# Recurrent attention beside a long convolution: five score blocks instead of eight, transposes in accumulator banks, and a larger resident part of one weight chunk

## The chip, the cores and the metric

The kernel runs on one core of a Trainium2 chip. The metric is the device time of one launch in microseconds. The profile comes from one execution of the same program; its times start at the first instruction, and the engines are named TensorE (PE, with its weight loads as PEld), VectorE (DVE), ScalarE (ACT), GpSimd (POOL) and SyncE (SP), which issues most of the loads.

## The reference: what is computed

Two independent halves are written side by side into one output of 2048 x 2048.

Half A is a gated long convolution: `k` is convolved with four taps per channel, multiplied by `v`, convolved over 2048 positions with a filter per channel by Fourier transforms, and multiplied by `q`.

Half B is a recurrence over 64 segments:

```python
for s in range(n_seg):                       # 64 segments of 32 rows
    xs = x[:, s * seg_len:(s + 1) * seg_len, :].copy()
    h = jnp.concatenate([mem, xs], axis=1)   # 8 memory rows + 32 rows = 40 rows
    q = jnp.einsum('btd,dhe->bhte', h, Wq)   # 32 heads of 128
    k = jnp.einsum('btd,dhe->bhte', h, Wk)
    v = jnp.einsum('btd,dhe->bhte', h, Wv)
    scores = jnp.einsum('bhqe,bhke->bhqk', q, k) * scale
    scores = jnp.where(mask[None, None], scores, -1000000000.0)
    p = _softmax(scores, axis=-1)
    o = jnp.einsum('bhqk,bhke->bhqe', p, v)
    o = jnp.einsum('bhte,hed->btd', o, Wo)
    mem = o[:, :M, :].copy()                 # the next segment's memory
    outs.append(o[:, M:, :])
```

A segment can't begin before the last one's first 8 output rows are known. Its weights are 4 matrices of 1024 x 4096 in bf16, 32 MB in all, and they do not fit into the on-chip memory; what does not fit is loaded again in each segment.

## The kernel before, in words

**Stages.** The first 460 us do half A on all engines, and, in its gaps, what of half B does not depend on the recurrence: the keys, queries and values of the last 8 rows of all 64 segments (each segment's 32 rows are kept as 24 and 8, and with the memory rows make up 32 + 8 of the 40). The results go to HBM tensors (`REC`, `VBD`) and come back segment by segment. Resident weight chunks are loaded at the end of this stage. Then comes the loop over 64 segments, whose instructions are written out in the order in which each engine runs them (`tc.manual_schedule()`): within an engine nothing overtakes, and waits across engines are put in by the framework from the tiles that an instruction reads and writes.

**Weights.** The matrices are cut into 64 chunks of 128 x 2048 (512 KB). `ORDER` is the order in which a segment uses them; 16 of them (`STREAM`) are streamed through a ring of five buffers `wring`. `fetch` issues the next load on SP as soon as `done` has freed a buffer. Two streamed chunks (`KEPT_A`, `KEPT_B`) are loaded once and kept in unused words of PSUM, out of which VectorE copies quarters into SBUF in each segment (`quarter`, `quarter_b`; line 796). One chunk, `PART`, has its first 512 columns resident in `part`; the other 1536 are loaded in each segment (line 722).

**One segment.** The 32 heads are done in two groups of 16, g = 0 and 1.

1. The keys and queries of group 0 are projected into two PSUM banks `acc0` and `acc1` (`Proj.run`, line 948: a chunk is four matmuls that run side by side), copied to SBUF by ScalarE (`evac`, line 957), transposed on TensorE into a bank of their own, `tps` (lines 889, 966), and copied out by VectorE (lines 1066, 1070).
2. The scores go to `S`, 8 blocks of 40 columns: blocks 0 to 3 hold the first 32 queries, four heads each; blocks 4 to 7 hold the last 8 queries of four heads stacked in the rows, so that in each row only one of the four blocks is the row's own head.
3. `softmax_a`: VectorE takes the maximum over all 8 blocks (981) and subtracts it (983), writes the mask into `S` for the next scores (`seed_scores`, 917 and 918), and ScalarE takes the exponential (986).
4. `softmax_b`: sum, reciprocal, multiplication with `rowhead` (1 for the row's own head, else 0), products into `P_pad`, a sum over the four blocks (1003), and four 32 x 32 transposes into `PT` (1008, 1009).
5. Group 1 does the same, interleaved: while VectorE works on group 0's softmax, TensorE projects q1 and then the first chunks of the values. The k1 transposes go to `tps`, the q1 transposes to `acc1` under the name `turned`; ScalarE copies both out (1079, 1082).
6. `attend` multiplies P with the values into `OTp`, ScalarE copies the result out (`evac_o`, 1028), and the output projection (1038) adds it into `yacc` in the banks `acc0` and `acc1`. `Y` is copied out (1128), stored, and its first 8 rows become the next memory (`fill_mem`, 898, 900).

On ScalarE, the order around the two softmaxes is what the code says: q1's evacuation stands behind the first exponential, and the copy of group 0's attention output behind the second:

```python
            E1 = softmax_a()
            pv1 = Proj(2, 1).run(3)
            attend(0, PT0, V0)
            OT0 = evac_o(0)
            PT1 = softmax_b(E1)
```

**POOL** issues DMAs of its own: in the first stage the loads of `v`, copies of streamed chunks and the stores of the x rows (`x_block`, line 604), in the loop `rec`, `VBs` and the output. The descriptors of these DMAs are kept in an SBUF area whose size `SCRATCH` sets.

Of the kernel before, what the change touches and what calls it, by code (L numbers as in the profile page):

```python
# [23 lines left out]
PART = (3, 4, 0)  # L24
# [14 lines left out]
SCRATCH = 1024  # L39
# [383 lines left out]
def b_kernel(ctx: ExitStack, tc, x, mem0, Wq, Wk, Wv, Wo, outb, n_seg, run_a):  # L423
# [168 lines left out]
    def x_block(b):  # L592
# [11 lines left out]
        rec_stores.append(nc.gpsimd.dma_start(REC[:, 4 * b:4 * b + 4, 0:256], xt.rearrange("p s k t -> p s (k t)")))  # L604
# [110 lines left out]
    def fetch():  # L715
        if loads:
            s, ch = loads.pop(0)
            live[s, ch] = k, t = slot()
            if ch in kept:
                nc.sync.dma_start(dst_view(t[:], ch), dram_chunk(ch))  # L720
            elif ch == PART:
                nc.sync.dma_start(t[:, 512:2048], stream_src(ch)[:, 512:2048])
            else:
                nc.sync.dma_start(t[:], stream_src(ch))
# [14 lines left out]
    with c0p:  # L739
# [16 lines left out]
        for g in range(2):  # L756
# [13 lines left out]
            if g == 0:  # L770
# [9 lines left out]
    two = ctx.enter_context(tc.tile_pool(name="b_two", bufs=2, side="right", reuse_waits="tile"))  # L780
# [10 lines left out]
    B_rest = one.tile([128, 192], I32, name="B_rest")  # L791
    B_homes = [[(tpi[:, 1, :], 0)], [(SBi[:, 320:448], 0), (OTi[:, :, 480:512], 128)], [(OTi[:, :, 416:480], 0)],
               [(B_rest[:], 0), (SBi[:, 448:512], 192)]]
# [7 lines left out]
    def quarter_b(q, tag):  # L801
        t = one.tile([128, 256], I32, tag=tag, name="quarter_b")
        w = []
        for home, at in B_homes[q]:
            n = home.shape[1] * (home.shape[2] if len(home.shape) == 3 else 1)
            if home.shape == B_rest[:].shape:
                part = home.bitcast(BF)
            else:
                bits(like(t[:, at:at + n], home), home)
                part = t[:].bitcast(BF)[:, 2 * at:2 * at + 2 * n]  # L810
# [35 lines left out]
    def pieces(ch):  # L846
# [4 lines left out]
        if ch == PART:  # L851
            return [(0, 512, part[:]), (512, 2048, live[now[0], ch][1][:, 512:2048])]
# [19 lines left out]
    part = one.tile([128, 512], BF, name="part")  # L872
    nc.sync.dma_start(part[:], dram_chunk(PART)[:, 0, 0:512])
# [30 lines left out]
    with tc.manual_schedule():  # L904
# [17 lines left out]
        for s in range(n_seg):  # L922
# [37 lines left out]
            def transposes(sb, tiles=False, tp=tps[:, 0, :]):  # L960
# [18 lines left out]
            def softmax_a():  # L979
                mx = two.tile([128, 8], F32, tag="mx", name="mx")  # L980
                nc.vector.tensor_reduce(out=mx[:], in_=S, op=ALU.max, axis=AX.X)  # L981
                E = one.tile([128, 8, 40], F32, tag="E", name="E")
                nc.vector.tensor_tensor(out=E[:], in0=S, in1=mx[:].unsqueeze(2).to_broadcast([128, 8, 40]),  # L983
                                        op=ALU.subtract)
                seed_scores()
                nc.scalar.activation(E[:], E[:], ACT.Exp, scale=scale)  # L986
                return E

            def softmax_b(E):
                ssum = two.tile([128, 8], F32, tag="ssum", name="ssum")  # L990
                nc.vector.tensor_reduce(out=ssum[:], in_=E[:], op=ALU.add, axis=AX.X)
                nc.vector.reciprocal(ssum[:], ssum[:])
                nc.vector.tensor_tensor(out=ssum[:, 4:8], in0=ssum[:, 4:8], in1=rowhead[:], op=ALU.mult)
                nc.vector.tensor_tensor(out=P_pad[:, 0:4, 0:32], in0=E[:, 0:4, 0:32],
                                        in1=ssum[:, 0:4].unsqueeze(2).to_broadcast([128, 4, 32]), op=ALU.mult)
                own = P_pad[:].rearrange("p b k -> p (b k)")[:, 32:320].rearrange("p (i w) -> p i w", w=72)
                nc.vector.tensor_tensor(out=own[:, 0:4, 0:8], in0=E[:, 0:4, 32:40],
                                        in1=ssum[:, 0:4].unsqueeze(2).to_broadcast([128, 4, 8]), op=ALU.mult)
                nc.vector.tensor_tensor(out=E[:, 4:8, :], in0=E[:, 4:8, :],
                                        in1=ssum[:, 4:8].unsqueeze(2).to_broadcast([128, 4, 40]), op=ALU.mult)  # L1000
                nc.vector.tensor_copy(P_pad[:, 4, 32:64].rearrange("p (i t) -> p i t", i=4), E[:, 4:8, 32:40])
                with nc.allow_low_precision("one of the four terms is not zero"):
                    nc.vector.tensor_reduce(out=P_pad[:, 4, 0:32], in_=E[:, 4:8, 0:32].rearrange("p i k -> p k i"),
                                            op=ALU.add, axis=AX.X)
                PT = one.tile([128, 2, 4, 40], BF, tag="PT", name="PT")
                for kb in range(2):
                    ks = slice(32 * kb, 32 * kb + 32)
                    nc.vector.transpose(out=PT[:, kb, :, 0:32], in_=P_pad[:, 0:4, ks])
                    nc.vector.transpose(out=PT[:, kb, :, 32:40], in_=P_pad[:, 4, ks])
                return PT  # L1010

            def attend(g, PT, V):
                for i in range(4):
                    cv = slice(i * 128, i * 128 + 128)
                    for c in range(4):
                        nc.tensor.matmul(OTp[:, c, i * 40:i * 40 + 40], lhsT=V[32 * c:32 * c + 32, cv],
                                         rhs=PT[32 * c:32 * c + 32, 0, i, :], start=(i == 0), stop=False,
                                         tile_position=(32 * c, 0), skip_group_check=True)
                for c in range(4):
                    nc.tensor.matmul(OTp[:, c, 0:160], lhsT=VBs[32 * c:32 * c + 32, g, :],  # L1020
                                     rhs=PT[32 * c:32 * c + 32, 1].rearrange("p i q -> p (i q)"), start=False, stop=True,
# [42 lines left out]
            q0.run(4)  # L1064
            KT0 = keys(0)
            nc.vector.tensor_copy(KT0[:, :, :, 0:32], transposes(k0, True))  # L1066
            q0 = q0.run(2).evac()
            k1 = Proj(0, 1).run(4)
            QT0 = one.tile([128, 4, 4, 32], BF, tag="QT", name="QT")
            nc.vector.tensor_copy(QT0[:], transposes(q0, True))  # L1070
# [8 lines left out]
            nc.scalar.copy(KT1[:, :, :, 0:32], transposes(k1))  # L1079
            turned = transposes(q1, tp=bank(1, "turned")[:].bitcast(BF)[:, 0:512])  # L1080
# [122 lines left out]
```

## Time and profile before

| | us |
|---|---|
| runs | 1789.31, 1791.54, 1793.37 (median 1791.54) |
| the profiled execution: its own time | 1793.29 |
| its span, first to last instruction | 1791.4 |
| TensorE busy | 1681.0 |
| VectorE busy | 1038.7 |
| ScalarE busy | 658.8 |
| GpSimd busy | 301.2 |
| moved by DMA | 623.31 MB, mean 348 GB/s |

A line of the timeline reads: start, duration, engine, line of the kernel, operation, output<-inputs, shapes, number of merged instructions, and in brackets the idle time of the engine before it with what ended it. A line of the waits reads: who waited for whom, microseconds in total, number of times, the longest. Matmul durations are of one instruction in a pipeline: the next starts before the last has ended, so the step from start to start is what a matmul takes of TensorE's time.

### The profile page before, as it was taken

The page shows a single profiled execution, that of the slowest core. Times are in us where ns is not written, and L with a number is a line of the kernel's source. Part 1 is how long each engine was busy: PE and PEld are TensorE (multiplying, and loading weights), DVE is VectorE, ACT ScalarE, POOL GpSimd, SP SyncE. Part 2 cuts the span into 40 slices and gives each one's busy share as a digit, 9 for nine tenths or more (in the row PEclk, how much of TensorE's full clock was granted, in tenths as well). Part 3 has the DMA queues.
Part 4 walks back from the last instruction along what each step waited for, and adds up shares of the span by engine and source line. Part 5 has one row for each costly group of instructions (what it writes and reads, how often), then busy time and mean ns, then how long its engine had stood idle before and what let it go on. Part 6 is the DMA issues. An engine that isn't in the chain of part 4 may idle for free.

```text
span 1791.4 us, 70833 instructions
## 1 busy us (share of the span) xinstructions
PE 1681.0 (94%) x30776; PEld 994.8 (56%) x30776; DVE 1038.7 (58%) x3429; ACT 658.8 (37%) x1157; POOL 301.2 (17%) x563
## 2 busy tenths in 40 slices
PE   6989997798999999999999999999999999999998
PEld 2443333343566666656666666665666666666665
DVE  9926875433555555555555555565555555656555
ACT  6955650001333333333333333333333333333333
POOL 4002342100111111111111111111111111111111
PEclk9999998899999999999999999999999999999999
DMA  9989987998999999999999999999999999999998
GB/s 342 361 324 290 308 285 265 337 315 325 381 359 356 352 369 372 358 350 364 359 359 368 347 363 354 367 366 352 345 355 365 364 363 350 375 362 364 369 364 295
DMA packets 219756, 623.31 MB, mean 348 GB/s; under 512 B 57442, under 2 KB 57586, under 8 KB 219444
## 3 DMA queue, kind: packets, MB, share of 16 engines
q1 hardware_dynamic: 160948, 550.58, 83.6%
q0 software_dynamic: 19104, 45.13, 7.4%
q10 hardware_dynamic: 39392, 23.07, 4.3%
q8 instruction: 241, 3.95, 0.9%
q14 instruction: 71, 0.58, 0.1%
HBM read 563.63 MB, written 57.67 MB: 347 GB/s over the span
## 4 chain that ended last, share of the span: by engine, by line
PE 66%; DMA 19%; DVE 6%; ACT 4%; issue 3%; ACTq 1%; POOL 0%; SPq 0%; POOLq 0%; DVEq 0%
PE acc L948 30%; PE yacc L1038 19%; DMA wring<-WS 14%; PE kb_ps L624 5%; DMA REC<-stage 2%; ACT OT L1028 2%; PE tps L889 2%; ACT s_sb L249 1%; DVE E L983 1%; DVE mx L981 1%; PE tps L966 1%; PE s_ps L247 1%; ACTq L653 1%; PE turned L966 1%; PE vb_ps L765 1%
## 5 line engine op out<-in xcount | busy, mean ns | idle before, releaser
L1038 PEld LDWEIGHTS <-OT 128*64 128x64 bf16 x8255 | 438.8, 109 | 53.6 <-ACT OT L1028 35.6
L948 PEld LDWEIGHTS <-rec 128*32 128x32 bf16 x12288 | 293.7, 96 | 291.3 <-DVE rec L900 41.7
L957 ACT CAST qkv_sb<-acc 128x512 bf16<-128x512 f32 x384 | 224.7, 585 | 514.1 <-PE acc L948 353.0
L948 PE MATMUL acc<-Wres,rec 128*32 128x512 bf16 x3328 | 242.6, 380 | 2.6 <-issue 2.1
L948 PE MATMUL acc<-wring,rec 128*32 128x512 bf16 x2300 | 228.2, 382 | 17.2 <-DMA wring<-WS 14.0
L1038 PE MATMUL yacc<-Wmore,OT 128*64 128x256 bf16 (+1 forms) x2560 | 219.9, 274 | 0.0
L948 PE MATMUL acc<-Wmid,rec 128*32 128x512 bf16 x3072 | 211.3, 379 | 1.0 <-issue 1.0
L1038 PE MATMUL yacc<-wring,OT 128*64 128x256 bf16 x2448 | 194.9, 273 | 6.9 <-DMA wring<-WS 6.9
L1130 POOL DMA_DIRECT2D out_dram<-Y x128 | 64.6, 507 | 487.4 <-ACT Y L1128 484.4
L796 DVE TENSOR_SCALAR quarter<-OTp 128x256 int32<-128x256 int32 x252 | 99.9, 417 | 78.4 <-ACT OT L1028 78.4
L1128 ACT CAST Y<-yacc 128x256 bf16<-128x256 f32 x128 | 47.6, 372 | 256.8 <-DVE quarter_b L796 164.8
L1028 ACT CAST OT<-OTp 128x640 bf16<-128x640 f32 x128 | 87.4, 683 | 143.4 <-PE OTp L1020 143.4
L948 PE MATMUL acc<-pw,rec 128*32 128x512 bf16 x1796 | 132.7, 379 | 1.0 <-issue 1.0
L1066 DVE COPY KT<-tps 128x512 bf16<-128x512 bf16 x64 | 27.2, 425 | 155.0 <-PE tps L889 155.0
L900 DVE CAST rec<-tps 128x32 bf16<-128x32 f32 x128 | 24.5, 192 | 159.1 <-PE tps L898 155.7
L948 PE MATMUL acc<-Wlate,rec 128*32 128x512 bf16 x1536 | 116.4, 379 | 0.0
L884 POOL DMA_DIRECT2D rec<-REC x64 | 36.2, 565 | 448.4 <-PE acc L948 432.7
L981 DVE TENSOR_REDUCE mx<-SB 128x8 f32<-128x320 f32 x128 | 62.9, 492 | 67.1 <-PE SB L975 64.0
L986 ACT ACTIVATE E<-E 128x320 f32<-128x320 f32 x128 | 60.1, 470 | 82.0 <-DVE E L983 82.0
L624 PE MATMUL kb_ps<-XBT,pw 128*128 128x512 bf16 x320 | 82.9, 400 | 1.9 <-DMA pw<-in_B_Wk_dram 1.3
L1038 PE MATMUL yacc<-Wlate,OT 128*64 128x256 bf16 x1024 | 79.1, 276 | 5.4
L932 POOL COPY KT<-rec 128x128 bf16<-128x128 bf16 x128 | 38.8, 303 | 227.2 <-PE SB L975 220.6
(223 smaller groups left out, 2671.5 us busy)
## 6 DMA issues: line engine op xcount, KB each, us to landing
wring<-WS SPq DMA_DIRECT2D x831, 512.0 KB, 6.2
wring<-WS SPq DMA_DIRECT2D x64, 384.0 KB, 5.7
rec<-REC POOLq DMA_DIRECT2D x64, 192.0 KB, 5.7
SK<-s_sb SPq DMA_DIRECT2D x16, 512.0 KB, 4.5
SU<-s_sb SPq DMA_DIRECT2D x16, 512.0 KB, 5.7
Kg<-SK SPq DMA_DIRECT2D x32, 256.0 KB, 4.1
Ug<-SU SPq DMA_DIRECT2D x32, 256.0 KB, 5.5
REC<-stage ACTq DMA_DIRECT2D x16, 512.0 KB, 13.2
```

Of the source, the lines that this page charges most:

```text
L624: nc.tensor.matmul(ps[:], lhsT=ws[kc][:, hl * 128:(hl + 1) * 128], rhs=xbt(kc).rearrange("p s t -> p (s t)"), start=(kc == 0), stop=(kc == 7))
L796: nc.vector.tensor_scalar(out=dst, in0=src, scalar1=0, scalar2=None, op0=ALU.bitwise_or)
L884: nc.gpsimd.dma_start(rec[:], REC[:, s, :])
L932: nc.gpsimd.tensor_copy(KT[:, :, :, 32:40], KBs[:, 128 * g:128 * g + 128].rearrange("p (c i t) -> p i c t", c=4, i=4))
L948: nc.tensor.matmul(self.acc[32 * c:32 * c + 32, :], lhsT=hT[:, ch[1], :], rhs=w[:, 512 * c:512 * c + 512], start=(ch == chs[0]), stop=(ch ...
L957: nc.scalar.copy(sb[:], self.acc[:])
L981: nc.vector.tensor_reduce(out=mx[:], in_=S, op=ALU.max, axis=AX.X)
L986: nc.scalar.activation(E[:], E[:], ACT.Exp, scale=scale)
L1028: nc.scalar.copy(OT[:], o_view)
L1038: nc.tensor.matmul(yacc[f][64 * dh:64 * dh + m, x - o:y - o], lhsT=lhsT, rhs=r, start=(h == (0, 2 * FIRST[-1])[f] and x == o), stop=stop, ...
L1128: nc.scalar.copy(Y[:, 256 * f:256 * f + 256], yacc[f][:, 0:256])
L1130: nc.gpsimd.dma_start(bass.AP(outb.tensor, outb.offset + SEG * s * 2048 + 512 * dh, [[2048, 32], [1, 512]]), Y[64 * dh + NM:64 * dh + 40, :])
```

## The change

Four things are changed together.

- **Resident part.** `part` holds 1280 of the 2048 columns of chunk `PART` instead of 512 (two loads ahead of the loop instead of one), and the load in each segment fetches 768 columns instead of 1536. `part` grows by 1536 bytes per partition.
- **Space for it.** The words `B_rest` (768 bytes), which held the rest of `KEPT_B`'s last quarter in SBUF, go: these 192 words now lie in `tps`, in the columns that the transposes used, and are copied out in each segment as the other quarters are. The descriptor area shrinks from 1024 to 512 bytes, for which the store in `x_block` is cut in two. `E` shrinks from 320 to 256 columns and takes in the small tiles of the softmax.
- **Transposes.** k0's go to bank 0 and q0's to bank 1, each after its own evacuation; the group is `q0.run(2)`, `k0.run(4)`, `q0.run(3)`, k0's transposes, `q0.run(3)`, where it was `run(4)` and `run(2)`. k1's and q1's go to the two halves of bank 1.
- **Softmax.** The four blocks of the last queries are multiplied with `rowhead` and summed into block 4 ahead of the maximum, and the rest of the softmax works on 5 blocks. P is transposed by two instructions instead of four, with `PT` laid out as [head, key half] instead of [key half, head].

```diff
-PART = (3, 4, 0)
+PART, PART_COLS = (3, 4, 0), 1280
-SCRATCH = 1024
+SCRATCH = 512
...
-        rec_stores.append(nc.gpsimd.dma_start(REC[:, 4 * b:4 * b + 4, 0:256], xt.rearrange("p s k t -> p s (k t)")))
+        for h in (0, 2):
+            rec_stores.append(nc.gpsimd.dma_start(REC[:, 4 * b + h:4 * b + h + 2, 0:256],
+                                                  xt[:, h:h + 2].rearrange("p s k t -> p s (k t)")))
...
-                nc.sync.dma_start(t[:, 512:2048], stream_src(ch)[:, 512:2048])
+                nc.sync.dma_start(t[:, PART_COLS:2048], stream_src(ch)[:, PART_COLS:2048])
...
-    B_rest = one.tile([128, 192], I32, name="B_rest")
-               [(B_rest[:], 0), (SBi[:, 448:512], 192)]]
+               [(tpi[:, 0, 64:256], 0), (SBi[:, 448:512], 192)]]
...
-    part = one.tile([128, 512], BF, name="part")
-    nc.sync.dma_start(part[:], dram_chunk(PART)[:, 0, 0:512])
+    part = one.tile([128, PART_COLS], BF, name="part")
+    nc.sync.dma_start(part[:, 0:1024], dram_chunk(PART)[:, 0, :])
+    nc.sync.dma_start(part[:, 1024:PART_COLS], dram_chunk(PART)[:, 1, 0:PART_COLS - 1024])
...
-            def transposes(sb, tiles=False, tp=tps[:, 0, :]):
+            def transposes(sb, bank_of, at=0, tiles=False):
+                tp = bank_of[:].bitcast(BF)[:, at:at + 512]
...
             def softmax_a():
-                nc.vector.tensor_reduce(out=mx[:], in_=S, op=ALU.max, axis=AX.X)
-                nc.vector.tensor_tensor(out=E[:], in0=S, in1=mx[:].unsqueeze(2).to_broadcast([128, 8, 40]),
-                                        op=ALU.subtract)
+                nc.vector.tensor_tensor(out=own, in0=S[:, 4:8, :], in1=rowhead[:].unsqueeze(2).to_broadcast([128, 4, 40]),
+                                        op=ALU.mult)
+                nc.vector.tensor_reduce(out=S[:, 4, :], in_=own.rearrange("p i k -> p k i"), op=ALU.add, axis=AX.X)
+                nc.vector.tensor_reduce(out=mx, in_=S[:, 0:5, :], op=ALU.max, axis=AX.X)
+                nc.vector.tensor_tensor(out=e, in0=S[:, 0:5, :], in1=mx.unsqueeze(2).to_broadcast([128, 5, 40]),
+                                        op=ALU.subtract)
                 seed_scores()
-                nc.scalar.activation(E[:], E[:], ACT.Exp, scale=scale)
+                nc.scalar.activation(e, e, ACT.Exp, scale=scale)
...
-                for kb in range(2):
-                    ks = slice(32 * kb, 32 * kb + 32)
-                    nc.vector.transpose(out=PT[:, kb, :, 0:32], in_=P_pad[:, 0:4, ks])
-                    nc.vector.transpose(out=PT[:, kb, :, 32:40], in_=P_pad[:, 4, ks])
+                nc.vector.transpose(out=PT[:, :, :, 0:32], in_=P_pad[:, 0:4, :])
+                nc.vector.transpose(out=PT[:, :, :, 32:40].rearrange("p i k t -> p k i t"), in_=P_pad[:, 4, :])
...
-            q0.run(4)
+            q0.run(3)
             KT0 = keys(0)
-            nc.vector.tensor_copy(KT0[:, :, :, 0:32], transposes(k0, True))
-            q0 = q0.run(2).evac()
+            nc.vector.tensor_copy(KT0[:, :, :, 0:32], transposes(k0, bank(0, "turned"), tiles=True))
+            q0 = q0.run(3).evac()
             k1 = Proj(0, 1).run(4)
-            nc.vector.tensor_copy(QT0[:], transposes(q0, True))
+            nc.vector.tensor_copy(QT0[:], transposes(q0, bank(1, "turned"), tiles=True))
...
-            nc.scalar.copy(KT1[:, :, :, 0:32], transposes(k1))
-            turned = transposes(q1, tp=bank(1, "turned")[:].bitcast(BF)[:, 0:512])
+            turned = bank(1, "turned")
+            nc.scalar.copy(KT1[:, :, :, 0:32], transposes(k1, turned))
+            turned = transposes(q1, turned, 512)
```

## The prediction

> **What bounds the kernel now.** I read the page first: TensorE carries the chain, with a DMA share.
>
> ```profile
> PE 1681.0 (94%) x30776; PEld 994.8 (56%) x30776; DVE 1038.7 (58%) x3429; ACT 658.8 (37%) x1157; POOL 301.2 (17%) x563
> ...
> PE 66%; DMA 19%; DVE 6%; ACT 4%; issue 3%; ACTq 1%; POOL 0%; SPq 0%; POOLq 0%; DVEq 0%
> ```
>
> Then the stages by windows. The columns are the stretch, its length, the busy times, the granted clock, the DMA share and GB/s.
>
> ```profile
> 0.00:460.00 460.00, 389.88 (x2249) 164.95 (x2253) 283.70 (x595) 183.30 (x275) 96.68 (x121) 0.94 0.91 317
> 460.00:800.00 340.00, 329.86 (x7300) 211.38 (x7296) 191.98 (x721) 121.05 (x225) 54.13 (x117) 1.00 0.98 361
> 1130.00:1460.00 330.00, 320.49 (x7076) 205.76 (x7064) 183.87 (x688) 116.20 (x216) 51.25 (x111) 1.00 0.98 359
> ```
>
> The recurrent loop holds 1327 of 1791 us. There TensorE is 97% busy and the DMA engines 98%: two resources near their ends. The waits from 460 us on tell which one ends last:
>
> ```profile
> PEld L1038 <- ACT OT L1028: 35.0, 61, 0.9
> ...
> PE acc L948 <- DMA wring<-WS: 12.3, 21, 1.1
> ...
> PE yacc L1038 <- DMA wring<-WS: 4.1, 8, 1.2
> ```
>
> TensorE waits only 16.4 us in all for streamed weights, while the loads on SP mostly wait for TensorE to free a ring slot. So TensorE sets the pace and the stream follows closely. The first segment of that timeline has no stream wait: 20.32 us between its two second-half Y copies (459.84 and 480.16 us). The mean of 63 segments is (1787.1 − 459.84)/63 = 21.07 us. The excess, 0.75 us a segment or 47 us, is all that a lighter stream could give back. What a new wait on TensorE costs is read from this segment:
>
> ```profile
> 462.30 0.58 ACT L957 CAST qkv_sb<-acc 128x512 bf16<-128x512 f32 x1 [2.09 <-PE acc L948]
> 462.66 0.39 PE L948 MATMUL acc<-wring,rec 128*32 128x512 bf16 x4
> ...
> 462.94 0.41 PE L889 MATMUL tps<-ident,qkv_sb 128*32 128x128 bf16 x16
> ...
> 463.39 0.42 DVE L1066 COPY KT<-tps 128x512 bf16<-128x512 bf16 x1 [2.31 <-PE tps L889]
> 463.60 0.82 PE L948 MATMUL acc<-Wmid,rec 128*32 128x512 bf16 x12
> ...
> 467.09 0.47 ACT L986 ACTIVATE E<-E 128x320 f32<-128x320 f32 x1 [0.61 <-DVE E L983]
> ...
> 467.74 0.58 ACT L957 CAST qkv_sb<-acc 128x512 bf16<-128x512 f32 x1 [0.18 <-PE acc L948]
> ...
> 468.27 0.40 PE L966 MATMUL tps<-ident,qkv_sb 128*128 128x128 bf16 x4
> ...
> 468.50 0.39 PE L966 MATMUL turned<-ident,qkv_sb 128*128 128x128 bf16 x4
> ...
> 468.75 0.58 ACT L1079 COPY KT<-tps 128x512 bf16<-128x512 bf16 x1 [0.43 <-PE tps L966]
> ...
> 471.38 0.47 ACT L986 ACTIVATE E<-E 128x320 f32<-128x320 f32 x1 [0.60 <-DVE E L983]
> ...
> 471.75 0.67 ACT L1028 CAST OT<-OTp 128x640 bf16<-128x640 f32 x1
> ...
> 472.48 0.63 PE L1038 MATMUL yacc<-Wlate,OT 128*64 128x256 bf16 x8
> ```
>
> One chunk of a projection (four matmuls side by side) occupies TensorE for about 0.22 us here (463.60 to 464.25 is three). From an engine's end to the start that it releases, these rows show some 0.05 us. Of the evacuations, the OT copy ends at 472.42 and TensorE starts at 472.48: already a stall, and it starts right behind the second exponential (471.38 to 471.75). So what delays that exponential delays TensorE one for one.
>
> **The change, part by part (per segment).**
>
> *First transposes, one chunk earlier and in accumulator banks.* The k0 transposes need the k0 evacuation, which ends at 462.88; today a chunk at 462.66 covers that. Now they come where that chunk stood and still start at 462.94. Three chunks follow (463.17 to 463.82), then k1 starts in bank 0, which VectorE's KT copy reads until 463.81: start 463.86 instead of 463.60. Part of it is won back, since the q0 transposes today wait for their evacuation: theirs would start at 464.73 instead of 464.52. Cost 0.21 us; bounds 0.15 (no wait for bank 0) and 0.28 (nothing won back).
>
> *Second transposes, both in bank 1.* The k1 transposes (468.27) went to a bank of their own. Now they need bank 1, thus the q1 evacuation, whose end at 468.32 plus 0.05 gives 468.37: 0.10 us. That evacuation stands behind the first exponential on ScalarE. ScalarE is free for it at 467.09 + 0.37 (the step from the second exponential to the OT copy) = 467.46, 0.28 before it starts. The exponential's start moves by 0.52 and its length shrinks by 0.10 (next part but one), so 0.14 us of that shows. Cost 0.24; bounds 0.10 and 0.40.
>
> *The q1 transposes behind the KT copy.* In the listing of the changed kernel's instructions, the q1 transposes wait for the ScalarE count that the KT copy of k1 reaches, though they write the other half of the bank. In before they wait for nothing late: 468.50 follows 468.27 directly. The KT copy starts 0.48 after the transposes that it reads and takes 0.58; with 0.05 for the release the second four start 1.11 after the first, not 0.23. Everything behind is queued on TensorE: five chunks of pv0, the scores, pv1. Cost 0.88; bounds 0.80 and 0.95. That one bank is guarded as a whole is also seen in before: VectorE's quarter copies of OTp's upper columns wait for ScalarE's OT copy of the lower ones (78.4 us, 63 times). The Trainium skill, PSUM — Partial Sum Buffer, section "PSUM bank collisions raise a hardware error", asks for this: guard by bank and quadrant, not by address. The trace agrees by those 63 waits; guarded by address this part would cost nothing and the sum would be 55 us lower.
>
> *Softmax, front.* Max (0.492) and subtract (0.491) over 320 columns go. In come: a product of 160 columns out of PSUM (0.328, as the seed of 160), a reduce of 160 to 40 (the 128-to-32 one took 0.368; 32 more columns at the 1.07 ns that 0.319 for 160 and 0.491 for 320 give: 0.40), max and subtract over 200 (0.36 each, 120 columns less). Two instructions more bring two more gaps of 0.03. The exponential starts 1.45 + 0.12 = 1.57 after the scores instead of 1.05: 0.52 later, and is 0.10 shorter (at 0.83 ns a column, from ScalarE's 372 ns for 256 and 585 for 512). The OT copy and TensorE's first output matmul behind it are 0.42 later; bounds 0.30 (reduce at the price of a plain 160) and 0.60 (its strided write to PSUM costs more).
>
> *Softmax, back.* Sum and product shrink, four instructions of 0.16 to 0.37 go, two small ones of about 0.17 come, and the four transposes (0.90) become two, which I put at 0.7. The chain gets some 0.7 us shorter, but it frees nothing: the second P is used at 474.78, 0.27 after its last transpose, and attention of group 0 waits for V's evacuation, not for P. Shorter work there costs and gives 0; were the cover gone it would be a loss only if the front's 0.52 exceeded it.
>
> *Kept quarter.* 192 words now need a VectorE copy (0.25 for 128, so 0.32), just ahead of the 64-word copy at 478.46. Both end near 479.0, the matmul reading them starts at 479.34: 0, as long as that 0.3 us lasts.
>
> *Stream.* The partial chunk loads 192 KB instead of 384 KB: one SP load as before, 12.6 MB less over 64 segments. Nothing moves at TensorE beyond its stream waits, plus fetch and queue stalls that the 98% share may cause. What it returns lies between the 16 named and the whole excess of 47 us; with a slower TensorE the share falls to about 0.9, so I take 28, the named ones and somewhat under half of the rest.
>
> *Ahead of the loop.* POOL issues 16 more stores (0.78 us each today, halves near 0.6): 6 us of an engine that idles there between Yre products. SP's part load becomes two and waits for VectorE's last output product rather than TensorE, about 1.5 us later, with the 13 Wv loads queued behind it; the loop's entry waits for stores and Wlate loads from 381 us on, which cover that. Half the descriptor space shows in no row; POOL's issues there keep 7 us and more apart for the most part. I take +1, between −3 and +8.
>
> **Sum.** 0.21 + 0.24 + 0.88 + 0.42 = 1.75 us; 63 segments give 110 (bounds 1.35 and 2.23: 85 and 140; the first segment waits for loads anyway). 110 − 28 + 1 = +83. The profiled execution took 1793.29 us (span 1791.4), 1.75 above the median 1791.54, and 1793.3 + 83 − 1.7 = 1875 us. Measured runs spread by 0.2%, so that is what counts as no change.
>
> **Rivals.**
>
> *Bytes set the time (faster).* The DMA engines are 98% busy at 358 to 361 GB/s in the loop. If transfers were the bound, 12.6 MB less at 360 GB/s would give 35 us: 1757 us. This decides if the added TensorE waits stay inside time that it now spends on the stream, some 0.26 us a segment; they come to 1.75. Against it also: a slice of the page at 381 GB/s, and the segment of 20.32 us. Chance 0.04. The Trainium skill, DMA: Bandwidth & Descriptors, section Specifications, puts the HBM limit of a core near 358 GB/s; by that the 12.6 MB are worth 35 us too, and the loop's rate agrees with the figure, the 381 of that slice does not.
>
> *The KT copy does not hold the q1 transposes.* Then 0.87 remains: 55 − 28 + 1 = +28, 1820 us. For it: the halves are disjoint. Against: the count in the listing. Chance 0.06.
>
> *Longer than forecast.* The strided reduce into PSUM or the restarts of TensorE cost more and little of the stream's excess comes back: 140 − 16 + 8 = +132, about 1922 us. Chance 0.08.
>
> **How the numbers follow.** The forecast has 0.82, its own range 1845 to 1912. Bounds taken against each other give 85 − 47 − 3 = +35 (1826) at the low end; the range 1838 to 1915 leaves out the faster rival, the KT one and part of the long one. Slower by over 0.2%: 0.95; faster 0.04; same 0.01.
>
> **What would show it.** The q1 transposes named as waiting for ScalarE's KT copy, near 0.9 us each; k1's transposes waiting for the q1 evacuation; the wait of L1038's weights for OT near 1.0 us instead of 0.57; stream waits under 5 us; segments near 22.4 us; the loop's rate near 330 GB/s. Wrong it would be if the q1 transposes follow k1's within 0.25 us, or if segments with no added TensorE waits set the end.

## The result, and the profile after

The changed kernel takes 1939.06 us (median; 1934.62 to 1944.53) against 1792.45 us for the kernel before on the same chip: a ratio of 1.0816, 95% interval 1.0778 to 1.0855. The direction was forecast, the size was not: 1939 lies above the range of 1838 to 1915.

The page of the changed kernel gives the busy times and the chain:

```profile
PE 1706.1 (88%) x30776; PEld 1004.7 (52%) x30776; DVE 1034.4 (53%) x3236; ACT 640.1 (33%) x1157; POOL 312.5 (16%) x579
...
PE 53%; DVE 11%; ACT 9%; DMA 7%; issue 5%; ACTq 1%; POOL 1%; SPq 0%; POOLq 0%; DVEq 0%
```

TensorE's share of the chain fell from 66% to 53%, DMA's from 19% to 7%, and what came instead is VectorE, ScalarE and issue. To see where the 146.8 us between the two profiled executions (1940.06 and 1793.29) come from, the span is cut at the end of the first segment, which is the end of the second second-half `Y` copy of ScalarE in the timeline, as in the prediction. It lies at 534.2 us instead of 460.2: **+74 us ahead of the loop**. The 63 segments behind it take 22.22 us in the mean instead of 21.07: **+73 us in the loop**. The shortest segments, which have no stream wait, went from 20.31 to 22.17 us, by 1.86; what the mean has above them (the excess) went from 0.76 to 0.05 us.

The windows of the changed kernel show both halves (stretch, its length, busy times, granted clock, DMA share, GB/s):

```profile
0.00:460.00 460.00, 345.13 (x1598) 134.82 (x1599) 251.30 (x520) 175.16 (x260) 104.77 (x132) 0.87 0.77 264
800.00:1130.00 330.00, 305.55 (x6733) 195.85 (x6729) 176.65 (x621) 108.20 (x209) 48.84 (x105) 1.00 0.94 333
```

In the loop TensorE waits more and the DMA engines move 333 instead of some 360 GB/s, as forecast. In the first 460 us everything fell: TensorE did 345 instead of 390 us of work, the DMA engines moved 264 instead of 317 GB/s. The waits of the changed kernel from 100 to 540 us say who stopped:

```profile
POOL REC L605 <- issue: 55.5, 14, 5.6
PE z_ps L375 <- POOL Yre L366: 48.8, 12, 9.0
...
POOL out_dram L418 <- issue: 19.4, 5, 6.1
...
POOL WS L675 <- issue: 12.2, 4, 6.1
```

The three "issue" rows stand for 87 us in which POOL stood ahead of a DMA of its own with nothing in the profile that it waited for. Before, from 0 to 540 us, there were no such rows for `REC` and `out_dram` and 2.0 us for `WS`, and TensorE waited 2.7 us for `Yre`. POOL's timeline around one block of x shows it, first before and then after:

```profile
162.49 1.15 POOL L366 TENSOR_TENSOR Yre<-pa,pb 128x512 bf16<-128x512 bf16 x1 [1.97 <-DVE pb L361]
165.05 0.78 POOL L604 DMA_DIRECT2D REC<-xt  x1 [1.41 <-DVE xt L603]
165.83 0.55 POOL L679 DMA_DIRECT2D WS<-pw  x1
166.40 1.17 POOL L366 TENSOR_TENSOR Yre<-pa,pb 128x512 bf16<-128x512 bf16 x1
```

```profile
161.67 1.16 POOL L366 TENSOR_TENSOR Yre<-pa,pb 128x512 bf16<-128x512 bf16 x1 [2.97 <-DVE pb L361]
164.12 0.73 POOL L605 DMA_DIRECT2D REC<-xt  x1 [1.29 <-DVE xt L603]
170.06 0.73 POOL L605 DMA_DIRECT2D REC<-xt  x1 [5.21 <-issue]
170.79 0.57 POOL L681 DMA_DIRECT2D WS<-pw  x1
171.38 2.27 POOL L366 TENSOR_TENSOR Yre<-pa,pb 128x512 bf16<-128x512 bf16 x2
```

The second half of the store starts 5.94 us after the first. The trace also tells when each DMA landed. For the first half, which starts at 164.12 us (least, median and longest are of this one store):

```profile
DMA to landing us min/median/max: 5.6/5.6/5.6
```

It landed at 169.75 us, and the second half starts 0.31 us later. The same holds for all 23 waits of the three rows: each ends 0.30 to 0.34 us after the landing of the last POOL DMA that was still on its way. Behind the second half in POOL's order stand the products `Yre`, and TensorE waits for these: 46 us more in named waits than before. How the rest of the 74 us comes about was not traced.

In the loop, the waits of the changed kernel from 460 us to the end answer to those shown of before:

```profile
PEld L1036 <- ACT OT L1026: 69.2, 64, 1.1
...
PE turned L965 <- ACT KT L1078: 46.6, 64, 0.7
PE yacc L1036 <- ACT OT L1026: 37.6, 64, 0.6
...
PE turned L965 <- ACT qkv_sb L955: 12.5, 54, 0.2
...
PE acc L946 <- DMA wring<-WS: 2.3, 4, 1.0
```

The wait for the `OT` copy was 35.0 us before, the stream's 12.3, and the two rows of `turned` are new. One segment's timeline after, in the rows that the prediction costed:

```profile
651.75 0.33 DVE L981 TENSOR_TENSOR E<-SB,rowhead 128x160 f32<-128x160 f32 x1 [0.63 <-PE SB L974]
652.11 0.45 DVE L983 TENSOR_REDUCE SB<-E 128x40 f32<-128x160 f32 x1
652.60 0.37 DVE L984 TENSOR_REDUCE E<-SB 128x5 f32<-128x200 f32 x1
653.00 0.37 DVE L985 TENSOR_TENSOR E<-SB,E 128x200 f32<-128x200 f32 x1
653.40 0.37 ACT L988 ACTIVATE E<-E 128x200 f32<-128x200 f32 x1 [1.20 <-DVE E L985]
653.68 0.57 ACT L955 CAST qkv_sb<-acc 128x512 bf16<-128x512 f32 x1
...
654.30 0.38 PE L965 MATMUL turned<-ident,qkv_sb 128*128 128x128 bf16 x4 [0.24 <-ACT qkv_sb L955]
654.77 0.59 ACT L1078 COPY KT<-turned 128x512 bf16<-128x512 bf16 x1 [0.53 <-PE turned L965]
655.41 0.38 PE L965 MATMUL turned<-ident,qkv_sb 128*128 128x128 bf16 x4 [0.73 <-ACT KT L1078]
```

The exponential starts 1.65 us after the first VectorE operation; k1's transposes start 0.05 us after q1's evacuation (653.68 + 0.57), and q1's follow 1.11 us later, 0.05 after the `KT` copy.

### The profile page after: what moved, and what is told of

Read it like the earlier page. It is cut to its first block, busy times and chain, and to the rows that moved or that the text cites. A ratio compares the mean times of both kernels' runs of the same rounds, so it can differ in the third digit from the quotient of the medians.

```text
span 1938.3 us, 70724 instructions
## 1 busy us (share of the span) xinstructions
PE 1706.1 (88%) x30776; PEld 1004.7 (52%) x30776; DVE 1034.4 (53%) x3236; ACT 640.1 (33%) x1157; POOL 312.5 (16%) x579
## 4 chain that ended last, share of the span: by engine, by line
PE 53%; DVE 11%; ACT 9%; DMA 7%; issue 5%; ACTq 1%; POOL 1%; SPq 0%; POOLq 0%; DVEq 0%
PE yacc L1036 23%; PE acc L946 19%; ACT qkv_sb L955 3%; DMA wring<-WS 3%; DVE SB L983 3%; PE turned L965 3%; DVE E L984 2%; DVE E L985 2%; ACT OT L1026 2%; DVE E L981 2%; ACT KT L1078 2%; PE turned L887 2%; DMA REC<-stage 2%; PE kb_ps L626 1%; ACT E L988 1%
## 5 line engine op out<-in xcount | busy, mean ns | idle before, releaser
L1036 PEld LDWEIGHTS <-OT 128*64 128x64 bf16 x8255 | 438.3, 109 | 78.1 <-ACT OT L1026 69.2
L946 PE MATMUL acc<-Wres,rec 128*32 128x512 bf16 x3328 | 236.3, 380 | 0.2 <-issue 0.2
L1036 PE MATMUL yacc<-Wmore,OT 128*64 128x256 bf16 (+1 forms) x2560 | 219.1, 274 | 0.0
L1036 PE MATMUL yacc<-wring,OT 128*64 128x256 bf16 x2256 | 187.0, 273 | 1.6 <-DMA wring<-WS 1.6
L1036 PE MATMUL yacc<-Wlate,OT 128*64 128x256 bf16 x1024 | 78.8, 276 | 37.6 <-ACT OT L1026 37.6
L981 DVE TENSOR_TENSOR E<-SB,rowhead 128x160 f32<-128x160 f32 x128 | 41.5, 324 | 129.1 <-PE SB L974 129.1
L1064 DVE COPY KT<-turned 128x512 bf16<-128x512 bf16 x64 | 27.2, 425 | 147.2 <-PE turned L887 147.2
L965 PE MATMUL turned<-ident,qkv_sb 128*128 128x128 bf16 x512 | 49.1, 217 | 59.6 <-ACT KT L1078 46.6
L988 ACT ACTIVATE E<-E 128x200 f32<-128x200 f32 x128 | 47.3, 370 | 151.2 <-DVE E L985 151.2
```

The costliest lines, as they stand in the source:

```text
L946: nc.tensor.matmul(self.acc[32 * c:32 * c + 32, :], lhsT=hT[:, ch[1], :], rhs=w[:, 512 * c:512 * c + 512], start=(ch == chs[0]), stop=(ch ...
L965: nc.tensor.transpose(dst, src, ident[:])
L981: nc.vector.tensor_tensor(out=own, in0=S[:, 4:8, :], in1=rowhead[:].unsqueeze(2).to_broadcast([128, 4, 40]), op=ALU.mult)
L988: nc.scalar.activation(e, e, ACT.Exp, scale=scale)
L1036: nc.tensor.matmul(yacc[f][64 * dh:64 * dh + m, x - o:y - o], lhsT=lhsT, rhs=r, start=(h == (0, 2 * FIRST[-1])[f] and x == o), stop=stop, ...
```

## The experiments

The theory after the result: (A) the half outside the loop is the room for POOL's descriptors; (B) the half in the loop is the sum of four TensorE waits that the prediction listed. The rivals: the cut stores themselves, as 16 more issues; one of the waits not being what it seems; and, for the stream, that a lighter stream is what gave time back. The table holds what the timelines of all kernels give: the end of the first segment, the mean of the 63 others, the shortest value that recurs among them, and what the means have above it in all (63 times the difference). The time is the median of the runs; the segments are those of the one profiled execution, whose own time is up to 7 us off that median (1864.20 for e1, 1780.53 for e12, 1771.08 for e11). So means that differ by less than some 0.1 us are not told apart by it, and the first segment's end lies between 459 and 465 us in kernels whose first stage is that of before (before, e6, e8, e11, e12).

| kernel | time, us | runs | first segment ends | mean | shortest | above it |
|---|---|---|---|---|---|---|
| before (profiled) | 1793.29 | 1 | 460.2 | 21.07 | 20.31 | 48 |
| after (profiled) | 1940.06 | 1 | 534.2 | 22.22 | 22.17 | 3 |
| e1_small_ring | 1857.44 | 2 | 534.1 | 21.02 | 20.31 | 45 |
| e2_cut_stores | 1791.32 | 8 | 464.0 | 20.98 | 20.31 | 42 |
| e3_after_ring | 1873.83 | 4 | 466.6 | 22.25 | 22.17 | 5 |
| e4_turns_first | 1895.01 | 1 | 531.2 | 21.56 | 21.48 | 5 |
| e5_ot_first | 1916.57 | 1 | 534.9 | 21.84 | 21.53 | 20 |
| e7_old_softmax | 1915.52 | 1 | 536.0 | 21.81 | 21.50 | 19 |
| e6_less_stream | 1788.48 | 10 | 460.0 | 20.96 | 20.31 | 41 |
| e12_small_load | 1786.94 | 10 | 459.0 | 20.89 | 20.31 | 36 |
| e11_one_load_fewer | 1765.46 | 4 | 464.8 | 20.64 | 20.31 | 21 |
| e8_before_ot_first | 1793.88 | 7 | 461.9 | 21.01 | 20.41 | 38 |
| e9_otp_turns | 1802.19 | 7 | 465.4 | 21.16 | 20.87 | 18 |
| e10_otp_ot_first | 1793.35 | 7 | 461.2 | 20.97 | 20.22 | 47 |

### e1_small_ring and e2_cut_stores: the area, and the stores alone

Both start from the kernel before. e1 has the small area and the cut stores, e2 the cut stores alone; the loop is untouched.

```diff
-SCRATCH = 1024
+SCRATCH = 512            # e1 alone
...
-        rec_stores.append(nc.gpsimd.dma_start(REC[:, 4 * b:4 * b + 4, 0:256], xt.rearrange("p s k t -> p s (k t)")))
+        for h in (0, 2):     # e1 and e2
+            rec_stores.append(nc.gpsimd.dma_start(REC[:, 4 * b + h:4 * b + h + 2, 0:256], ...
```

> The kernel before with only the descriptor area halved (512 bytes) and the x-row stores cut in two; stream, transposes and softmax as before. Theory A (room for descriptors): POOL's second half store waits some 5 us for the first to drain, the Yre products and all behind it are late, and the first segment ends near 534 us instead of 460; the segments stay at 21.07 us; in all about 1866 us (between 1850 and 1880), with over 40 us of POOL's waits ahead of these stores that no engine's work ends. Theory B (the stage's other changes: the larger part load, its wait on VectorE, another interleaving): first segment ends by 470, in all 1790 to 1803 us.

> The kernel before with the x-row stores cut in two, the descriptor area left at 1024 bytes. Theory A (room): 16 more issues of about 0.7 us on an engine with idle time, first segment ends between 458 and 468 us, in all 1790 to 1800 us. Rival A2 (the number of POOL's DMA issues, not the room): first segment ends near 530, in all about 1862 us.

Against before, e1 has a ratio of 1.0405 (1.030 to 1.051), and its first segment ends at 534.1 us, where that of the changed kernel ends. e2 has 1.000 (0.997 to 1.003) and ends its first segment at 464.0. The waits of e1 from 100 to 540 us, and POOL's timeline of e2 around the same block:

```profile
POOL REC L605 <- issue: 57.7, 14, 9.1
...
PE z_ps L375 <- POOL Yre L366: 49.2, 12, 9.1
```

```profile
166.13 1.45 POOL L605 DMA_DIRECT2D REC<-xt  x2 [1.34 <-DVE xt L603]
167.57 0.57 POOL L681 DMA_DIRECT2D WS<-pw  x1
168.16 1.17 POOL L366 TENSOR_TENSOR Yre<-pa,pb 128x512 bf16<-128x512 bf16 x1
```

With the large area the same two halves go out one right behind the other (merged as x2, 1.45 us in all). So the +74 us belong to the size of the area, all of them that show (e2's 3.8 us lie within the spread of that stage), and the number of issues costs nothing that shows. The Trainium skill, DMA: Bandwidth & Descriptors, section "SWDGE vs HWDGE vs iDMA", says that GpSimd writes the descriptors of its DMAs into rings in an area of SBUF, which the DMA engines drain; the runs agree, in that the area's size alone decides whether POOL stands still ahead of these stores for 57.7 us or not at all. That POOL stands until an earlier store has landed is shown by the landing times of the changed kernel. How much the area holds was not measured; it does not go by the bytes of the transfer alone, since the 512 KB copy `WS` goes out right behind the second half of 128 KB.

### e3_after_ring: the changed loop without the small area

The changed kernel with 1024 bytes of area. For the space, `part` holds 1024 columns instead of 1280; the stores stay cut.

```diff
-PART, PART_COLS = (3, 4, 0), 1280
+PART, PART_COLS = (3, 4, 0), 1024
-SCRATCH = 512
+SCRATCH = 1024
```

> The changed kernel with the descriptor area back at 1024 bytes; to make room the resident part holds 1024 columns instead of 1280. Theory (the stage ahead of the loop is lost to room for descriptors alone): first segment ends between 458 and 470 us, the segments stay at 22.2 us, in all 1866 us (1855 to 1878). Rival (the stage is slow for the larger part load and its wait, or for the cut stores): first segment ends above 500 us, in all above 1900.

1873.83 us (1873.37 to 1876.03), ratio 1.0468 (1.0435 to 1.050). The first segment ends at 466.6 us, and the segments are those of the changed kernel, though the stream carries 64 KB more in each. What the area does not cause is 82 us over the 1791.33 of before here, against the forecast's +83. That it comes so close is in part luck: 74 of them are the loop's, for which 82 were forecast, and the first segment ends 6 us later than that of before.

### e4_turns_first: the q1 transposes ahead of the KT copy

The changed kernel; all eight transposes are issued before the copy, so that they no longer wait for it, while the copy now waits for all eight.

```diff
-            nc.scalar.copy(KT1[:, :, :, 0:32], transposes(k1, turned))
+            k1_turned = transposes(k1, turned)
             turned = transposes(q1, turned, 512)
+            nc.scalar.copy(KT1[:, :, :, 0:32], k1_turned)
```

> The changed kernel with the q1 transposes issued straight after k1's, ahead of ScalarE's KT copy, so that they no longer wait for it; the KT copy waits for them instead. Theory (the KT copy's hold of 0.88 us is the largest term of the loop): the q1 transposes follow k1's within 0.25 us, some 0.2 us comes back as a wait of the scores for the QT copy, segments of 21.5 us instead of 22.18 (21.4 to 21.7), the loop 43 us shorter, in all near 1896 us. Rival (the wait only moves to the scores): segments of 22.0 us or more.

The row of a segment in which the two groups of four stand as one:

```profile
712.98 0.61 PE L965 MATMUL turned<-ident,qkv_sb 128*128 128x128 bf16 x8
```

The shortest segment falls by 0.69 us to 21.48, the time by 44 us in one run. The hold is real, though the two halves of the bank are disjoint: it comes from the guard on the bank as a whole. The gain is less than 0.88, and ScalarE's steps tell why: the `KT` copy starts 0.23 us later, since it now waits for all eight transposes, and the step from the V evacuation to the second exponential grew by 0.19. The step from the `KT` copy to the V evacuation, in which the hold lay, fell by 1.11.

### e5_ot_first and e7_old_softmax: the softmax's share

e5 is the changed kernel with the copy of group 0's attention output ahead of the second exponential on ScalarE. e7 is the changed kernel with the softmax of before on 8 blocks (`part` at 1024 columns), P still transposed in two instructions.

```diff
-            E1 = softmax_a()
+            E1 = softmax_a(False)     # e5: without the exponential
             pv1 = Proj(2, 1).run(3)
             attend(0, PT0, V0)
             OT0 = evac_o(0)
+            nc.scalar.activation(E1[1], E1[1], ACT.Exp, scale=scale)
```

> The changed kernel with ScalarE's copy of group 0's attention output issued ahead of the second exponential. Theory (the output projection starts late because that copy stands behind an exponential which the longer softmax front delays): TensorE's first output matmul follows the last value chunk at once, the wait of L1036's weights for OT goes from 1.0 us to near 0 and segments to 21.5 us (21.4 to 21.65), in all near 1895 us. Rival (the softmax of group 1 is itself needed as early): attention of group 1 waits for P, and segments stay above 21.9 us.

> The changed kernel with the softmax of before (8 blocks, maximum and subtraction at once, selection behind), its transposes of P still two instructions; the resident part holds 1024 columns to make room. Theory (the longer front costs 0.42 us at the attention output's copy and 0.14 at the q1 evacuation, and the shorter back gives nothing): segments of 21.6 us instead of 22.18 (21.5 to 21.75), in all near 1902 us. Rival (the front's length is hidden, what it saves behind pays for it): segments of 22.1 us or more.

In e5 the shortest segment falls by 0.64 us, more than the 0.48 that the softmax had cost there, since the copy no longer stands behind an exponential at all. In e7 it falls by 0.67: so the five-block front costs about what was summed for it, 0.42 at the `OT` copy and 0.24 at the second transposes. But both means fall by 0.4 only, and so both forecasts of the segment (21.5 and 21.6) were met by the shortest ones alone. The waits of e5 from 460 us on:

```profile
PEld L1037 <- ACT OT L1027: 26.8, 63, 0.4
PE acc L946 <- DMA wring<-WS: 10.2, 23, 1.1
```

Two fifths of the gain came back as time above the shortest segment: the stream's named waits are back at 10.2 us, and that time at 20 us. e4, with shortest segments as long and the same stream, has 5 us there. Where in the segment TensorE waits seems to decide that; why was not settled.

### e6_less_stream, e12_small_load, e11_one_load_fewer: what a lighter stream returns

All three start from the kernel before. e6 loads 192 KB of the partial chunk instead of 384, e12 64 KB, e11 nothing; the missing columns are multiplied out of another resident chunk, with the same work on every engine.

```diff
-                nc.sync.dma_start(t[:, 512:2048], stream_src(ch)[:, 512:2048])
+                nc.sync.dma_start(t[:, 1280:2048], stream_src(ch)[:, 1280:2048])   # e6; e12: 1792:2048; e11: no load
-            return [(0, 512, part[:]), (512, 2048, live[now[0], ch][1][:, 512:2048])]
+            return [(0, 512, part[:]), (512, 1280, res[3, 5, 0][:, 512:1280]), (1280, 2048, live[now[0], ch][1][:, 1280:2048])]
```

> The kernel before with 192 KB less streamed in each segment and nothing else: columns 512 to 1279 of the partial chunk are not loaded, and another resident chunk's columns are multiplied in their place. Theory (TensorE sets the pace, the stream's return is bounded by the excess of 47 us over the shortest segment): segments of 20.4 to 20.75 us instead of 21.07, 20 to 42 us less, in all about 1760 us. Rival (the stream hardly holds the loop; only the 16 us of named waits come back): segments of 20.8 to 20.9 us, in all 1776 us.

> The kernel before without the load of the partial chunk in any segment: one load of fourteen and 384 KB less, columns 512 to 2047 of that chunk being multiplied from another resident chunk instead. Theory (what holds the mean above the shortest segment is the number of loads in turn through five buffers, each some 6 us from issue to landing, and not their bytes): a mean of 20.5 to 20.7 us instead of 21.0, 20 to 30 us less in all. Rival (it is neither: the excess comes from other fetches and queues): a mean of 20.85 or more, under 10 us less.

> The kernel before, with the load of the partial chunk kept but cut from 384 KB to 64 KB a segment (columns 512 to 1791 of it are multiplied out of another resident chunk, so this part of the output projection is computed with the wrong weights; the work per engine is the same). Two experiments are to be told apart by it: 192 KB less in the same load returned nothing (ratio 0.999), the whole load of 384 KB left out returned 22 us. Theory of the loads: what counts is that a load stands in the row of five buffers, and its bytes hardly count. Then 320 KB less return at most 5 us: about 1785 us, segments 20.9 us in the mean. Theory of the bytes, with a threshold: the stream has to get lighter by more than 192 KB before the stalls go. Then 64 KB left stand near the kernel without the load: about 1770 us, segments 20.7 us. The shortest segment stays at 20.31 us in both.

| left of the load | ratio to before, 95% interval | segments, mean |
|---|---|---|
| 384 KB (before) | 1 | 21.07 |
| 192 KB (e6) | 0.999 (0.997 to 1.001) | 20.96 |
| 64 KB (e12) | 0.998 (0.996 to 1.000) | 20.89 |
| no load (e11) | 0.988 (0.984 to 0.992) | 20.64 |

Half of the load taken away returned nothing that can be told from zero, less than either theory had put on it. Five sixths of its bytes taken away returned 0.2%, some 4 us, at the edge of what can be told from zero; the load left out returned 1.2%, some 22 us (14 to 28), so that the last 64 KB with the load itself are worth some 18. The rows of DMA issues of e12 (KB each, us to landing):

```profile
wring<-WS SPq DMA_DIRECT2D x831, 512.0 KB, 6.1
wring<-WS SPq DMA_DIRECT2D x64, 64.0 KB, 4.9
```

A load of 64 KB needs 4.9 us to land, one of 384 KB needed 5.7. So in this loop a load costs, and its bytes hardly. That it is its place in the row of five buffers that costs is argued, not shown: in e11 TensorE's named stream waits fell from 16.6 to 4.0 us, and the waits of its weight loads for nothing that the profile names fell too, while e12 has 13.9 and 35.9 us:

```profile
PEld L948 <- issue: 34.8, 60, 1.4
...
PEld L948 <- issue: 17.7, 27, 1.4
```

The first row is of before, the second of e11. What that second kind of wait stands for was not found. The DMA share does not tell the two apart: it is 0.97, at 349 GB/s, in e11's window from 800 to 1130 us, and the same in e12's:

```profile
800.00:1130.00 330.00, 324.15 (x7160) 209.79 (x7156) 190.09 (x717) 119.54 (x222) 51.53 (x111) 1.00 0.97 349
```

### e8, e9, e10: other places for the same work

e8 is the kernel before with e5's order on ScalarE. e9 is the changed kernel with the area at 1024, `part` at 1024 columns and whole stores, whose k0, q0 and k1 transposes go to the banks of `OTp`, so that neither an accumulator bank nor the `KT` copy holds TensorE; the projections have `run(4)` and `run(2)` again. e10 is e9 with e5's order.

```diff
-            nc.vector.tensor_copy(KT0[:, :, :, 0:32], transposes(k0, bank(0, "turned"), tiles=True))
-            q0 = q0.run(3).evac()
+            nc.vector.tensor_copy(KT0[:, :, :, 0:32], transposes(k0, OTp, tiles=True))
+            q0 = q0.run(2).evac()
...
-            nc.scalar.copy(KT1[:, :, :, 0:32], transposes(k1, turned))
+            nc.scalar.copy(KT1[:, :, :, 0:32], transposes(k1, OTp))
```

> The kernel before with ScalarE's copy of group 0's attention output issued ahead of the second exponential. Theory (the shortest segment is TensorE's own and this takes its wait of 0.27 us for the copy away, but the mean is held by loads' time from a freed buffer to landing, which does not depend on it): shortest segments of 20.05 us instead of 20.31, a mean of 20.9 to 21.05 instead of 21.0, 1785 to 1793 us. Rival (each removed TensorE wait shows in full): a mean of 20.75 to 20.8 us and 1774 to 1777 us.

> The changed kernel with the transposes of k0, q0 and k1 in the free columns of OTp's banks instead of the accumulators' (and k0's chunk order as before), the descriptor area at 1024 bytes, stores whole, the part at 1024 columns. Theory (the bank waits cost 0.21 + 0.24 + 0.88 us, of which only what the softmax's front adds stays): first segment ends near 462 us, segments of 20.9 us (20.75 to 21.1), in all about 1782 us. Rival (the copies out of four banks, or new waits on OTp, cost as much): segments above 21.5 us, in all above 1820.

> The changed kernel with k0's, q0's and k1's transposes in OTp's banks, the descriptor area at 1024 bytes, whole stores, a part of 1024 columns, and the copy of group 0's attention output ahead of the second exponential. Theory (as above: TensorE's own segment falls by the 0.65 us that this copy cost, the mean stops at what the loads allow): shortest segments of 20.25 us, a mean of 20.85 to 21.0, first segment's end near 465, 1783 to 1794 us. Rival (with 128 KB less streamed the loads follow): a mean of 20.45 to 20.6 us, 1757 to 1767 us.

| kernel | ratio to before, 95% interval |
|---|---|
| e8 | 1.0042 (1.0013 to 1.0070) |
| e9 | 1.0058 (1.0035 to 1.0082) |
| e10 | 1.0032 (1.0007 to 1.0058) |

e9's shortest segment is 20.87 us: of the 1.86 us that the change had added, 1.30 came from the banks into which the transposes were put and the chunk order that went with them, and 0.56 is left for the softmax. Its mean is 21.16 and its time 1802, where 20.9 and 1782 had been expected. e10's shortest segment is 20.22, below that of the kernel before, and yet its mean is 20.97 and its time no better: it has 47 us above its shortest segment, where e9 has 18. So there the gain of TensorE's own segment is lost above it. e8 tells less: it took 11 us off TensorE's wait for `OT` (35.0 to 23.8 us), but its shortest segment rose to 20.41 instead of falling to 20.05. By the medians of ScalarE's steps the `OT` copy starts 0.47 us earlier after the V evacuation, the evacuation behind it starts no earlier, since the exponential now stands between the two, and from there to the second `OT` copy it takes 0.10 us longer. None of the three beats the kernel before.

## Why the prediction was right in the loop and wrong in the sum

**The step that failed is "Ahead of the loop".** It said "Half the descriptor space shows in no row; POOL's issues there keep 7 us and more apart for the most part", and put +1 us, at most +8, on it. It measured +74, and e1 and e2 put all of it on the area: POOL stands until an earlier DMA has landed, 14 times 4 us in the `REC` row alone, with `out_dram` and `WS` behind. Neither half of that sentence holds. In before, 21 of the 41 intervals between POOL's DMAs from 100 to 460 us are under 7 us, 12 of them under 2 us. And the change itself puts two halves of a store back to back. The descriptor space also did show in one row of before:

```profile
POOL WS L673 <- issue: 2.0, 1, 2.0
```

This `WS` store, at 257.14 us, is the third DMA within 5 us, and starts 0.31 us after the first of them, a `REC` store, has landed. So the area of 1024 bytes, too, seems to have made POOL wait once. (Another row of this form, `POOL pw L575 <- issue: 14.7, 2, 9.4` in the first 100 us, is 13.1 us after; it isn't shown to have the same cause.) The whole `REC` stores of before need 6.0 us to land. The bound from the other side should have come from these: POOL in order, the second half of each store late by up to one landing, and the `Yre` products late with it.

**The four TensorE terms were right.** The steps between ScalarE's operations in the two timelines, medians over the segments, give each its size:

| step of the prediction | forecast, us | measured |
|---|---|---|
| First transposes (k0 to q0 evacuation: 1.58 to 1.80) | 0.21 | 0.22 |
| Second transposes (k1 evacuation to `KT` copy: 2.85 to 3.15) | 0.24 | 0.30 |
| q1 transposes behind the `KT` copy (`KT` copy to V evacuation: 1.43 to 2.32) | 0.88 | 0.89 |
| Softmax, front (V evacuation to `OT` copy: 1.57 to 2.05) | 0.42 | 0.48 |
| sum | 1.75 | 1.89 (shortest segment: 1.86) |

The front came out 0.06 larger since the reduce of 160 to 40 takes 0.45 instead of 0.40 us, and each operation on 200 columns 0.37 instead of 0.36; the exponential starts 1.65 instead of 1.57 us after the scores, and the second transposes carry a part of the same delay. Back and kept quarter cost nothing: no row of TensorE waits for `P` or `quarter_b`. By 46.6 us in 64 waits the trace agrees with the rule that the prediction took from the Trainium skill, PSUM — Partial Sum Buffer, section "PSUM bank collisions raise a hardware error", to guard by bank and not by address.

**"Stream" had a fair size for a wrong reason.** It forecast 28 us back, and 45 came (48 to 3). But not from the 192 KB: taken away alone (e6) they return at most 6 us (the lower end of its interval), and e3, with 64 KB more than the changed kernel in each segment, keeps the same 5 us above its shortest segment. That the time came back because TensorE became slower, so that each load has more time per segment, is the reading that is left, and not shown: no changed loop with the whole 384 KB was run, and e4 and e5, with segments of the same length, keep 5 and 20 us. In the sum, 117 (63 times 1.86) less 45 is 72, and the loop showed 73; forecast was 110 less 28. The terms were 7 us low and the return 17 us low; that the loop came within 10 us of its forecast is in part the luck of these two.

**The rivals.** "Bytes set the time" is refuted by e6 and e12: 12.6 MB less return not 35 us but none that show. "The KT copy does not hold the q1 transposes" is refuted by its own wait and by e4. "Longer than forecast" named 1922, from a dearer softmax and less stream return. The softmax came out 0.06 us dearer, 4 us in all, and the stream returned more, not less; the time came near 1922 by another way, which is luck.

**What would show it.** All six signs came: the waits for the `KT` copy (0.73 each, where 0.9 was named), those for the q1 evacuation (12.5 us in 54), `L1036`'s wait for `OT` (35.0 us in 61 waits before, 0.57 each; 69.2 in 64 after, 1.08), stream waits under 5 us (4.6), a loop at 333 GB/s and segments at 22.2 (22.4 named). None of them looked at the first 460 us, and that is where the half that was missed lay.

## What to carry to other kernels

When a change shrinks a resource that no row shows, price it by what its user would do if it ran out: who issues in order behind it, how long one transfer takes to land, and how often two stand back to back in the changed code. And a stream through a few buffers that follows its consumer closely can be paid by the load rather than by the byte: try to take a whole load out before cutting one. What is taken off the consumer's own waits can come back above its shortest segment, as in e10; whether it would stay with a load fewer was not run.

## What the hardware showed that was not expected

- POOL, with its DMA area halved, stood 5.2 us ahead of a 128 KB store that takes it 0.73 us to issue, and no semaphore in the profile names that wait: it reads "issue". In the changed kernel these waits end 0.3 us after the landing of an earlier DMA. Where one DMA follows another on POOL, such a row can mean that there is no room for the second.
- Cutting a load from 384 to 64 KB took 0.8 us off its time to land (5.7 to 4.9), and the share of busy DMA engines went only from 0.98 to 0.97 (800 to 1130 us).
- In the changed kernel, e1, e4, e5 and e7, all with the small area, TensorE's granted clock from 100 to 460 us was 0.82 to 0.84, against 0.91 to 0.95 in the nine kernels with the large one, while TensorE was less busy there (267 us of 360, instead of 311 in the kernel before). What of the 74 us that is was not taken apart.
- The sum of 160 columns into 40 took 0.43 to 0.45 us, where a product of as many took 0.33 and a maximum over 200 columns read in order 0.37. Whether its reading across the blocks or its write into PSUM costs that was not taken apart.
